# Weight blocks fetched in pairs, and the first units' decays in another order, in a recurrent attention kernel with an ELU network

## Chip, core, metric

The kernel runs on one core of a Trainium2 chip. The metric is the device time of one execution in microseconds (us). The profile is one execution, taken by the hardware profiler; its times count from the start of its span.

## What is computed

```
f = 1 / (1 + exp(-f_logit))                      # q, k, v, f: 4 x 8 x 768 x 48
for t in range(768):
    state = f[t] * state + outer(k[t], v[t])     # one 48 x 48 state for each of 4 x 8 heads
    y[t]  = q[t] @ state
x   = y with the heads side by side              # 3072 x 384
h   = x @ w_in                                   # w_in 384 x 2048
g   = where(h > 0, h, exp(min(h, 0)) - 1)
out = g @ w_out                                  # w_out 2048 x 384
```

All inputs are float32 but `w_in` and `w_out`, which are float64.

## The kernel before

The tokens are worked in 12 units of 256 (`U`), three for each batch. In a unit the recurrence is done in chunks of 64 tokens (`C`): `gates` makes 1 + exp(-f_logit) on ScalarE, `grow` multiplies it up along the tokens on VectorE (a scan), `fall` takes its reciprocal on VectorE (`nc.vector.reciprocal`, line 636), and `scale` multiplies k by the one and q by the other on GpSimd (POOL, line 626). `transposed` turns k over on TensorE, `advance` forms the state updates, `scores` the q-k products, `mask` keeps the causal ones (VectorE, line 722), `step` adds up the states (line 695), and `outputs` and `carried` (for unit 0 `first_outputs`, line 817) form x, which is copied out of PSUM as tile `xt` (lines 827 and 829).

The heads are in pairs p = 0 to 3. Pairs 0 to 2 hold 48 rows of each head at the partitions `MAIN`; the two heads of the fourth pair (index `NKT`) have their decays in the gaps at both ends of the partitions, and `move` brings them to their place by two DMAs from tile `f` to tile `f` (line 643). Only after that can k and q of that pair be scaled.

The network works on units too: for each pair of 128-wide column blocks j = 0 to 7, `up` (psH, line 949 for unit 0, line 904 for the others), `exped` and `elu` (line 958), and `down` (psM, lines 981 and 1015). One step T of the main loop is half a block: at even T `up` of block T / 2, at odd T `down` of a block two earlier. `at_step(T, ...)` puts other work at a step; the tables A1, A2, A3 and D2, D3 say at which. All runs in one order written out by hand (a manual schedule): each engine works its instructions in the order in which the program issues them.

The float64 weights are fetched into a staging tile `area` of 7 slots of 128 x 768 float64, and turned into float32 in three operations, in order of need n = 0 to 15 (w_in blocks 0, 1, 2, then w_out 0, w_in 3, w_out 1 and so on):

- `split(n)`: two VectorE operations (lines 568 and 572), the first into `bits`, the second in place
- `lower(n)`: one ScalarE activation in place (line 578)
- `merge(n)`: one VectorE operation into `wi` or `wo` (line 586), after which, in `fetch`, block n + 7 is fetched into the slot that has become free

A w_in block takes three DMAs (384 rows by 256 columns, runs of 2 KB: `MAIN` 576 KB, and twice 96 KB into the gaps), a w_out block one (768 KB). All come from SP's queue, in program order. Blocks 0 and 1 (`HOLD`) are fetched before unit 1's k, q and v are down; blocks 2 to 6 only after a small GpSimd memset of the staging slots (line 1142). A DMA that is issued takes one of eight completion semaphores in turn, on SP's queue and ACT's together, and waits until the last DMA on that semaphore has landed.

Later the slots of `area` serve again: for `combos` (sums of w_out, line 872) and `mixes` (sums of w_in, line 885), which units 1 to 11 use in place of some of the products.

Before the main loop stands the start-up: unit 0's whole recurrence, the decays of unit 1, and the first two weight blocks. `warm` issues products of an identity that nobody reads (psW, lines 1072 and 1074), whole ones or, by its third argument, tiny ones.

The start-up's last part, before:

```python
    fall(1, 0)
    split(0)
    for c in range(NC - 1):
        step(0, c)
    lower(0)
    mask(0, pc)
    step(0, NC - 1)
    fall(1, 1)
    split(1)
```

Of the kernel before, what the change touches and what calls it, by code (L numbers as in the profile page):

```python
# [356 lines left out]
def fast(ctx: ExitStack, tc: tile.TileContext, q, k, v, f_logit, w_in, w_out, out, flag, outer):  # L357
# [18 lines left out]
    nc = tc.nc  # L376
# [18 lines left out]
    LAG = 2  # L395
    AHEAD = 7
    WA = 1
    F1 = 3
    W0 = 3
    SMALL = 16  # L400
    MORE = 3
    RR = 2
    HOLD = 2
    A1 = (2, 8, 10, 11)
    D2 = (16, 18, 20, 22)
    A2 = (23, 25, 25, 26, 27, 28)
    D3 = (-7, -5, -3, -1)
# [60 lines left out]
    nc.scalar.preload_act_table(AF.Exp)  # L468
    blank(0, nc.vector, nc.gpsimd)
    blank(1, nc.vector, zeros=nc.gpsimd)  # L470
    load(0, "fkq")
    load(1, "f")
    load(0, "v")

    fine = cst.tile([128, NKT, 1], FP32, name="fine")
    nc.vector.memset(fine[:], 1.0)
# [39 lines left out]

    area = cst.tile([128, AHEAD, 2 * DM], w_in.dtype, name="area") if wide else None
    if wide:
        combos = [area[:, i].bitcast(FP32).rearrange("p (n f) -> p n f", f=DH) for i in (5, 6, 0, 1)]
    else:  # L520
        apart = cst.tile([128, 4, NP, DH], FP32, name="combos")
        combos = [apart[:, i] for i in range(4)]

    mixes = cst.tile([128, NP, 4, 128], FP32, name="mixes") if not wide else (
        area[:, 2:5].bitcast(FP32).rearrange("p a f -> p (a f)")[:, 0 : NP * 512]
        .rearrange("p (n c f) -> p n c f", n=NP, c=4)
    )

# [7 lines left out]
    )  # L536
    parts = [need[1:] for need in needs]

    def fetch(n):
        if n >= NFT:  # L540
            return
        j, out_ = parts[n]
        c = slice(j * 256, (j + 1) * 256)
        to = wo[:, 2 * j : 2 * j + 2] if out_ else wi[j][:]
        if wide:
            raws[n] = area[:, n % AHEAD]
            to = raws[n].rearrange("p (k f) -> p k f", k=to.shape[1])
        if out_:
            nc.sync.dma_start(out=to, in_=w_out[c, :].rearrange("(n p) f -> p n f", n=2))
            return  # L550
        nc.sync.dma_start(out=to[MAIN], in_=w_in[0 : NKT * 2 * D, c].rearrange("(k q) f -> q k f", k=NKT))
        rest = w_in[NKT * 2 * D :, c].rearrange("(r d k) f -> r d k f", r=2, d=PAD)
        for r in range(2):
            nc.sync.dma_start(out=to[GAP[r] : GAP[r] + PAD], in_=rest[r])

    held = {}

# [19 lines left out]
    def merge(n):  # L580
        if wide and n < NFT:
            hi = raws.pop(n).bitcast(I32)[:, 1::2]
            j, out_ = parts[n]
            to = wo[:, 2 * j : 2 * j + 2] if out_ else wi[j][:]
            bits, hi = (x.rearrange("p (k f) -> p k f", k=to.shape[1]) for x in (held.pop(n)[:], hi))
            nc.vector.tensor_tensor(out=to.bitcast(I32), in0=bits, in1=hi, op=ALU.add)
        fetch(n + AHEAD)

# [23 lines left out]
    def gates(u, pieces=(NKT,), bias=1):  # L612

        p = 0
        for n in pieces:
            a = qkf[u % NB]["f"][:, p : p + n, 0]
            nc.scalar.activation(a, a, AF.Exp, scale=-1.0)
            if bias:
                nc.scalar.activation(a, a, AF.Copy, bias=1.0)
            p += n  # L620

    def scale(u, *todo):

        t = qkf[u % NB]
        for n, p, e in todo:
            e.tensor_tensor(out=t[n][:, p], in0=t[n][:, p], in1=t["f"][:, p, "kq".index(n)], op=ALU.mult)  # L626

    def grow(u, p):

        g = qkf[u % NB]["f"][:, p, 0]  # L630
        nc.vector.tensor_tensor_scan(out=g, data0=g, data1=g, initial=1.0, op0=ALU.mult, op1=ALU.max)

    def fall(u, p):

        f = qkf[u % NB]["f"]
        nc.vector.reciprocal(f[:, p, 1], f[:, p, 0])  # L636

    def move(u, which, queue):

        f = qkf[u % NB]["f"]  # L640
        for r in range(2):
            to = PAD + D * r
            queue.dma_start(out=f[to : to + D, NKT, which], in_=f[GAP[r] : GAP[r] + PAD, 0:NKT, which])

    def decays(u, p):
        grow(u, p)
        fall(u, p)
        scale(u, ("k", p, nc.gpsimd))
        if p:
            scale(u, ("q", p - 1, nc.gpsimd))  # L650
        if p == NKT - 1:
            move(u, slice(0, 2), nc.sync if u > 1 else nc.scalar)

    def watch(u):
        nc.vector.scalar_tensor_tensor(
# [421 lines left out]


    gates(0, (1, 2))
    fetch(0)  # L1080
    load(1, "kqv")
    for n in range(1, HOLD):
        fetch(n)
    warm(W0, "m3")
    for p in range(NKT):
        grow(0, p)
        scale(0, ("k", p, nc.gpsimd))
        if p < 2:
            transposed(0, 0, "m0", (p,))
    move(0, 0, nc.scalar)  # L1090
    transposed(0, 1, "m1", (0,))
    fall(0, 0)
    scale(0, ("q", 0, nc.gpsimd))
    warm(WA, "m3")
    gates(1, bias=0)
    advance(0, (0, 1))
    pc = scores(0, ("m2", "m3"), (0,))
    nc.gpsimd.tensor_copy(
        even_v[:, :, :, PAD:],
        vs[0][:, :, PAD : PAD + NKT * 2 * D].rearrange("t w (p r d) -> t w p r d", r=2, d=D)[:, :, :, 0],  # L1100
    )
    fall(0, 1)
    scale(0, ("k", NKT, nc.gpsimd), ("q", 1, nc.gpsimd))
    fall(0, 2)
    move(0, 1, nc.scalar)
    warm(4)
    transposed(0, 1, "m1", (1,))
    advance(0, (2,))
    scores(0, None, (1,), pc)
    scale(0, ("q", 2, nc.gpsimd))  # L1110
    advance(0, (3,))
    scores(0, None, (2,), pc)
    nc.gpsimd.tensor_copy(
        padded_v[:, :, :, PAD : 2 * PAD].rearrange("t w (r j) k -> t w r j k", r=2),
        vs[0][:, :, PAD + NKT * 2 * D : PAD + DM].rearrange("t w (r k j) -> t w r j k", r=2, j=NKT),
    )
    a = qkf[1]["f"][:, 0:NKT, 0]
    nc.vector.tensor_scalar_add(a, a, 1.0)
    for p in range(NKT):
        grow(1, p)  # L1120
    move(1, 0, nc.sync)
    scale(0, ("q", NKT, nc.gpsimd))
    warm(2)
    scores(0, None, (NKT,), pc)
    warm(1)
    fall(1, 0)
    split(0)
    for c in range(NC - 1):
        step(0, c)
    lower(0)  # L1130
    mask(0, pc)
    step(0, NC - 1)
    fall(1, 1)
    split(1)
    for c in range(NC - 1):
        nc.gpsimd.tensor_copy(
            padded_s[:, c, :, PAD : 2 * PAD],
            sts[0, c + 1][:, NKT * 64 + PAD : (NKT + 1) * 64].rearrange("p (k j) -> p j k", j=NKT),
        )

    if wide:
        nc.gpsimd.memset(area[:, HOLD:].bitcast(I32)[:, :, 0:1], 0)
    for n in range(HOLD, AHEAD):
        fetch(n)
    merge(0)
    first_outputs(0)
    first_outputs(1)
    lower(1)
    scale(1, ("k", 0, nc.gpsimd), ("q", 0, nc.gpsimd), ("k", 1, nc.gpsimd), ("k", 2, nc.gpsimd))
    scale(1, ("k", NKT, nc.gpsimd))  # L1150
    fall(1, 2)
    watch(0)
    watch(1)
    scale(1, ("q", 1, nc.gpsimd), ("q", 2, nc.gpsimd))
    at_step(A1[2], lambda: outputs(1, ("m3", "m0")), lambda: lower(A1[2]), lambda: lower(A1[2] + 1))
    for n in range(1, NFT):
        t = min(max(needs[n][0] - 2, 0), n) + 2 * (n == NFT - 1)
        if t != A1[1]:
            at_step(t, lambda n=n: merge(n))
        if n > 1:  # L1160
            later.setdefault(max(min(t, n) - 2, 0), []).append(n)
    at_step(F1, lambda: move(1, 1, nc.scalar))
    at_step(F1 + 2, lambda: scale(1, ("q", NKT, nc.gpsimd)))
    at_step(A1[0], lambda: transposed(1, 0, "a0"), lambda: transposed(1, 1, "a1"))
    at_step(4, lambda: warm(0, "m3", SMALL))
# [97 lines left out]
```

## Time and profile before

| | us |
|---|---|
| median of 3 runs | 559.49 (558.94 to 560.98) |
| the profiled execution | 559.46 |
| its span | 557.7 |
| start-up, to the first psH | 30.28 |
| TensorE busy in the span | 543.0 |
| VectorE busy in the span | 406.4 |
| mean granted clock of TensorE | 0.994 |

The span is what the profile's engines show; some 1.8 us lie around it. A line of the timeline gives start and length in us, engine, line of the program, operation, tile written and tiles read, and, in brackets, how long the engine had been idle and what released it. DMA is counted by its 16 engines' busy share and by the GB/s that they moved.

### The profile page before, as it was taken

The numbers are of one execution on the slowest core, as the hardware profiler recorded it, in microseconds if no ns is written. First come the engines' busy times: TensorE is split into PE (matmuls) and PEld (weight loads), VectorE is DVE, ScalarE is ACT, GpSimd is POOL, SyncE is SP. The second block draws the span as 40 slices with busy tenths as digits, with TensorE's granted clock in tenths as the row PEclk, the third lists the DMA queues.
The fourth block names the chain that finished last, engine by engine and source line by source line (L and its number), as shares of the span: only waits on it lengthen the run. The fifth ranks groups of instructions, "written<-read, shape, count | busy, mean of one in ns | idle before, by whom it ended". The sixth has DMA issues, their size and how long they took to land.

```text
span 557.7 us, 15617 instructions
## 1 busy us (share of the span) xinstructions
PE 543.0 (97%) x6358; PEld 507.9 (91%) x6358; DVE 406.4 (73%) x804; ACT 228.3 (41%) x443; POOL 287.8 (52%) x559
## 2 busy tenths in 40 slices
PE   7889999999999999999999999999999999999996
PEld 3477679999999999999999999999999999999996
DVE  8799888887676776786785785786686687745553
ACT  3279764333434343333434334343343344333331
POOL 6600786475473474375465366357258258325332
PEclk9899999999999999999999999999999999999998
DMA  8998971033035135216217207307307302301001
GB/s 211 261 264 214 278 184 43 4 84 88 3 82 146 30 76 149 63 34 186 68 22 186 81 9 192 87 8 192 86 9 191 88 9 72 88 5 33 31 2 35
DMA packets 39474, 54.30 MB, mean 97 GB/s; under 512 B 4032, under 2 KB 29216, under 8 KB 39392
## 3 DMA queue, kind: packets, MB, share of 16 engines
q1 hardware_dynamic: 38592, 52.61, 36.5%
q8 instruction: 52, 0.85, 0.6%
q10 hardware_dynamic: 800, 0.59, 0.4%
q14 instruction: 30, 0.25, 0.2%
HBM read 45.02 MB, written 4.72 MB: 89 GB/s over the span
## 4 chain that ended last, share of the span: by engine, by line
PE 91%; DMA 2%; DVE 2%; ACT 1%; POOL 1%; issue 1%; SPq 1%; ACTq 0%; DVEq 0%; POOLq 0%
PE psH L904 39%; PE psM L1015 37%; PE psM L981 3%; PE psH L949 2%; PE psY L752 2%; PE psY L772 2%; PE psU_a L737 2%; PE psS L714 2%; PE psT L674 1%; DMA area<-in_moe_w_out_dram 1%; DMA f<-f 1%; ACT area L578 1%; DVE f L636 1%; POOL q L626 1%; DMA f<-in_f_logit_dram 0%
## 5 line engine op out<-in xcount | busy, mean ns | idle before, releaser
L904 PE MATMUL psH<-xt,wi 128*128 128x128 f32 (+1 forms) x1056 | 195.0, 294 | 0.0
L968 POOL TENSOR_TENSOR sums<-gg 128x128 f32<-128x128 f32 x172 | 75.6, 460 | 207.8 <-DVE gg L958 188.1
L936 ACT ACTIVATE gg<-hh 128x512 f32<-128x512 f32 x88 | 55.5, 630 | 249.3 <-DVE hh L926 111.7
L904 PEld LDWEIGHTS psH<-xt,wi 128*128 128x128 f32 x1056 | 149.5, 192 | 1.6
L904 PE MATMUL psH<-xt,area 128*128 128x128 f32 x704 | 121.5, 275 | 0.0
L904 PEld LDWEIGHTS psH<-xt,area 128*128 128x128 f32 x704 | 106.5, 192 | 4.5
L913 DVE TENSOR_TENSOR hh<-psH,u 128x256 f32<-128x256 f32 x88 | 36.9, 419 | 97.8 <-ACT u L911 97.7
L1015 PE MATMUL psM<-area,sums 128*128 128x192 f32 x516 | 99.9, 326 | 0.0
L1015 PEld LDWEIGHTS psM<-area,sums 128*128 128x128 f32 x516 | 86.0, 190 | 0.3 <-issue 0.2
L1015 PE MATMUL psM<-wo,gg 128*128 128x192 f32 x376 | 77.7, 332 | 0.0
L958 DVE SCALAR_TENSOR_TENSOR gg<-gg,hh 128x512 f32<-128x512 f32 x88 | 63.8, 725 | 1.5 <-ACT gg L937 1.5
L636 DVE RECIPROCAL f<-f 128x256 f32<-128x256 f32 x36 | 62.7, 1747 | 1.3
L937 ACT ACTIVATE gg<-gg 128x512 f32<-128x512 f32 x96 | 60.6, 631 | 3.0
L1015 PEld LDWEIGHTS psM<-wo,gg 128*128 128x128 f32 x376 | 60.2, 190 | 1.3
L926 DVE TENSOR_TENSOR hh<-psH,u43h 128x256 f32<-128x256 f32 (+1 forms) x176 | 54.6, 352 | 3.0
L626 POOL TENSOR_TENSOR q<-q,f 128x256 f32<-128x256 f32 x48 | 39.6, 826 | 19.5 <-DMA f<-f 12.9
L968 POOL TENSOR_TENSOR sums<-gg,sums 128x128 f32<-128x128 f32 x86 | 45.4, 528 | 6.7
L626 POOL TENSOR_TENSOR k<-k,f 128x256 f32<-128x256 f32 x48 | 39.3, 821 | 10.2 <-DMA f<-f 8.3
L926 DVE TENSOR_TENSOR u43h<-psH,hh 128x256 f32<-128x256 f32 x88 | 37.0, 420 | 9.2 <-PE psH L904 8.7
L968 POOL TENSOR_TENSOR sums<-sums,gg 128x128 f32<-128x128 f32 x86 | 43.0, 500 | 0.0
L1015 PE MATMUL psM<-area,gg 128*128 128x192 f32 x172 | 42.0, 326 | 0.0
L1015 PE MATMUL psM<-wo,sums 128*128 128x192 f32 x172 | 42.0, 326 | 0.0
(102 smaller groups left out, 646.3 us busy)
## 6 DMA issues: line engine op xcount, KB each, us to landing
area<-in_moe_w_out_dram SPq DMA_DIRECT2D x8, 768.0 KB, 10.6
again<-in_moe_w_in_dram SPq DMA_DIRECT2D x16, 384.0 KB, 3.6
again<-in_moe_w_out_dram SPq DMA_DIRECT2D x16, 384.0 KB, 3.6
k<-in_k_dram SPq DMA_DIRECT2D x12, 384.0 KB, 4.5
q<-in_q_dram SPq DMA_DIRECT2D x12, 384.0 KB, 5.6
v<-in_v_dram SPq DMA_DIRECT2D x12, 384.0 KB, 5.8
area<-in_moe_w_in_dram SPq DMA_DIRECT2D x8, 576.0 KB, 8.3
out_dram<-o SPq DMA_DIRECT2D x42, 96.0 KB, 2.4
```

The costliest lines, as they stand in the source:

```text
L626: e.tensor_tensor(out=t[n][:, p], in0=t[n][:, p], in1=t["f"][:, p, "kq".index(n)], op=ALU.mult)
L636: nc.vector.reciprocal(f[:, p, 1], f[:, p, 0])
L714: nc.tensor.matmul(pc[r][FULL[b], w, p], lhsT=t["k"][FULL[r], p, cols], rhs=t["q"][FULL[r], p, cols], start=True, stop=True,)
L904: nc.tensor.matmul(to, lhsT=lhs, rhs=rhs, start=(n == 0), stop=True, skip_group_check=True)
L913: add = lambda to, x, y: nc.vector.tensor_tensor(out=to, in0=x, in1=y, op=ALU.add)
L926: add = lambda to, x, y: nc.vector.tensor_tensor(out=to, in0=x, in1=y, op=ALU.add)
L936: nc.scalar.activation(g[:], h, AF.Relu, scale=-1.0)
L937: nc.scalar.activation(g[:], g[:], AF.Exp, scale=-1.0)
L958: nc.vector.scalar_tensor_tensor(out=g[:], in0=g[:], scalar=-1.0, in1=phs.pop(P), op0=ALU.add, op1=ALU.max)
L968: nc.gpsimd.tensor_tensor(out=s[:, i], in0=x, in1=y, op=op)
L981: nc.tensor.matmul(pm[t][:], lhsT=g[:, i, t * 128 : (t + 1) * 128], rhs=wo[:, 2 * j + i, :], start=(j == 0 and i == 0), stop=(j == NP - 1 ...
L1015: nc.tensor.matmul(pm[bank][:, half * DH : (half + 1) * DH], lhsT=x, rhs=y, start=first, stop=(j == NP - 1), skip_group_check=True,)
```

## The change

- `fetch` is called by kind and block. w_in comes in pairs of blocks: three DMAs bring 96 rows by 512 columns each, into two neighbouring slots (runs of 4 KB in the weight, 2 KB in each slot), and four the gaps of both. A table gives each pair and each w_out block its slot; `combos` and `mixes` lie at other slots accordingly.
- The order of SP's transfers is another. Unit 0's v comes ahead of unit 1's f; no w_in goes out ahead of the first `move`; unit 1's k follows the first two pairs, then unit 1's `move`, w_out 0 and 1, unit 1's q and v, w_out 2, the third pair, w_out 3, the fourth pair. w_out 7 is fetched after the loads of unit 2, which are themselves issued at step 8 as before.
- The first `move` uses ACT's and SP's queue, one DMA each. The second (of the reciprocals of the fourth pair) is gone: `fall(0, NKT)` takes the reciprocal in place.
- All three `fall` of unit 1 come in the main loop (steps 1, 3 and 4), with the q products that follow them; before, one came after the first psH was due. Unit 1's second `move` is at step 4, unit 1's transposes at step 4 instead of 2.
- Unit 1's "+ 1" is an activation on ScalarE instead of a VectorE operation.
- `mask` and all `step` of unit 0 stand ahead of `split(0)` and `split(1)`. `merge(2)` is at step 1.
- Fewer whole `warm` products in the start-up (7 calls' worth instead of 11); two more tiny ones at step 4, three more at step 22. The memset is gone.

```diff
-    F1 = 3
+    F1 = 4
-    SMALL = 16
-    MORE = 3
+    SMALL = 18
+    MORE = 6
-    HOLD = 2
-    A1 = (2, 8, 10, 11)
+    A1 = (4, 8, 10, 11)
...
-    load(0, "fkq")
+    load(0, "fkqv")
     load(1, "f")
-    load(0, "v")
...
-        combos = [area[:, i].bitcast(FP32).rearrange("p (n f) -> p n f", f=DH) for i in (5, 6, 0, 1)]
+        combos = [area[:, i].bitcast(FP32).rearrange("p (n f) -> p n f", f=DH) for i in (3, 0, 1, 2)]
...
-        area[:, 2:5].bitcast(FP32).rearrange("p a f -> p (a f)")[:, 0 : NP * 512]
+        area[:, 4:7].bitcast(FP32).rearrange("p a f -> p (a f)")[:, 0 : NP * 512]
...
+    spots = {("in", 0): 0, ("in", 2): 2, ("in", 4): 0, ("in", 6): 2}
+    spots.update({("out", j): i for j, i in enumerate((4, 5, 6, 4, 5, 0, 1, 2))})
+
+    def fetch(kind, j):
+        i = spots[kind, j]
+        if kind == "out":
...
+            return
         if wide:
+            for h in range(2):
+                raws[parts.index((j + h, 0))] = area[:, i + h]
+            to, c = area[:, i : i + 2].rearrange("p h (k f) -> p k h f", k=NKT), slice(j * 256, (j + 2) * 256)
+            for k_ in range(NKT):
+                rows = slice(k_ * 2 * D, (k_ + 1) * 2 * D)
+                nc.sync.dma_start(out=to[MAIN, k_], in_=w_in[rows, c].rearrange("q (h f) -> q h f", h=2))
...
+    after = {
+        1: (("out", 2),), 5: (("in", 6), ("out", 4)), 8: (("out", 5), ("out", 6)), 12: (("out", 7),),
+    }
...
-        fetch(n + AHEAD)
+        for what in after.get(n, ()):
+            fetch(*what)
...
     gates(0, (1, 2))
-    fetch(0)
-    load(1, "kqv")
-    for n in range(1, HOLD):
-        fetch(n)
...
-    move(0, 0, nc.scalar)
+    move(0, 0, (nc.scalar, nc.sync))
+    fetch("in", 0)
+    fetch("in", 2)
+    load(1, "k")
+    for p in range(2):
+        transposed(0, 0, "m0", (p,))
...
-    gates(1, bias=0)
+    gates(1)
...
-    fall(0, 2)
-    move(0, 1, nc.scalar)
-    warm(4)
...
+    warm(1)
+    fall(0, NKT)
+    scale(0, ("q", NKT, nc.gpsimd))
+    scores(0, None, (NKT,), pc)
...
-    a = qkf[1]["f"][:, 0:NKT, 0]
-    nc.vector.tensor_scalar_add(a, a, 1.0)
-    for p in range(NKT):
-        grow(1, p)
-    move(1, 0, nc.sync)
-    scale(0, ("q", NKT, nc.gpsimd))
-    warm(2)
-    scores(0, None, (NKT,), pc)
-    warm(1)
-    fall(1, 0)
+    grow(1, 0)
+    mask(0, pc)
+    for c in range(NC):
+        step(0, c)
     split(0)
-    for c in range(NC - 1):
-        step(0, c)
-    lower(0)
-    mask(0, pc)
-    step(0, NC - 1)
-    fall(1, 1)
-    split(1)
+    grow(1, 1)
+    grow(1, 2)
+    move(1, 0, (nc.sync, nc.sync))
+    fetch("out", 0)
+    fetch("out", 1)
+    load(1, "qv")
...
-    if wide:
-        nc.gpsimd.memset(area[:, HOLD:].bitcast(I32)[:, :, 0:1], 0)
-    for n in range(HOLD, AHEAD):
-        fetch(n)
+    split(1)
+    first_outputs(0)
+    lower(0)
     merge(0)
-    first_outputs(0)
     first_outputs(1)
     lower(1)
...
-    fall(1, 2)
...
+    at_step(1, lambda: fall(1, 0), lambda: scale(1, ("q", 0, nc.gpsimd)), lambda: merge(2))
...
-    at_step(F1, lambda: move(1, 1, nc.scalar))
+    at_step(F1 - 1, lambda: fall(1, 1), lambda: scale(1, ("q", 1, nc.gpsimd)))
+    at_step(F1, lambda: fall(1, 2), lambda: scale(1, ("q", 2, nc.gpsimd)))
+    at_step(F1, lambda: move(1, 1, (nc.scalar, nc.scalar)), lambda: fetch("in", 4), lambda: fetch("out", 3))
```

More of the change, by code (lines that the diff above doesn't have):

```diff
@@ L537, in fast @@
     parts = [need[1:] for need in needs]
-    def fetch(n):
-        if n >= NFT:
+    spots = {("in", 0): 0, ("in", 2): 2, ("in", 4): 0, ("in", 6): 2}
[3 more added lines that the diff above has]
+        if kind == "out":
+            to = wo[:, 2 * j : 2 * j + 2]
+            if wide:
+                to = area[:, i].rearrange("p (k f) -> p k f", k=2)
+                raws[parts.index((j, 1))] = area[:, i]
+            nc.sync.dma_start(out=to, in_=w_out[j * 256 : (j + 1) * 256, :].rearrange("(n p) f -> p n f", n=2))
@@ L541, in fetch @@
             return
-        j, out_ = parts[n]
-        c = slice(j * 256, (j + 1) * 256)
-        to = wo[:, 2 * j : 2 * j + 2] if out_ else wi[j][:]
         if wide:
[L546 to L551, printed above, removed]
@@ L552, in fetch @@
-        rest = w_in[NKT * 2 * D :, c].rearrange("(r d k) f -> r d k f", r=2, d=PAD)
-        for r in range(2):
-            nc.sync.dma_start(out=to[GAP[r] : GAP[r] + PAD], in_=rest[r])
+            for h in range(2):
[4 more added lines that the diff above has]
+                nc.sync.dma_start(out=to[MAIN, k_], in_=w_in[rows, c].rearrange("q (h f) -> q h f", h=2))
@@ new lines, in fetch @@
+        for h in range(2):
+            to, c = area[:, i + h].rearrange("p (k f) -> p k f", k=NKT) if wide else wi[j + h][:], j + h
+            c = slice(c * 256, (c + 1) * 256)
+            if not wide:
+                nc.sync.dma_start(
+                    out=to[MAIN], in_=w_in[0 : NKT * 2 * D, c].rearrange("(k q) f -> q k f", k=NKT)
+                )
+            rest = w_in[NKT * 2 * D :, c].rearrange("(r d k) f -> r d k f", r=2, d=PAD)
+            for r in range(2):
+                nc.sync.dma_start(out=to[GAP[r] : GAP[r] + PAD], in_=rest[r])
@@ L636, in fall, with move @@
         nc.vector.reciprocal(f[:, p, 1], f[:, p, 0])
-    def move(u, which, queue):
+    def move(u, which, queues):
         f = qkf[u % NB]["f"]
@@ L642, in move @@
             to = PAD + D * r
-            queue.dma_start(out=f[to : to + D, NKT, which], in_=f[GAP[r] : GAP[r] + PAD, 0:NKT, which])
+            queues[r].dma_start(out=f[to : to + D, NKT, which], in_=f[GAP[r] : GAP[r] + PAD, 0:NKT, which])
     def decays(u, p):
@@ L651, in decays @@
         if p == NKT - 1:
-            move(u, slice(0, 2), nc.sync if u > 1 else nc.scalar)
+            move(u, slice(0, 2), (nc.sync, nc.sync))
     def watch(u):
@@ L1087, in fast @@
         scale(0, ("k", p, nc.gpsimd))
-        if p < 2:
-            transposed(0, 0, "m0", (p,))
-    move(0, 0, nc.scalar)
+    move(0, 0, (nc.scalar, nc.sync))
[4 more added lines that the diff above has]
+        transposed(0, 0, "m0", (p,))
     transposed(0, 1, "m1", (0,))
@@ L1101, in fast @@
     )
+    advance(0, (2,))
+    warm(1)
     fall(0, 1)
-    scale(0, ("k", NKT, nc.gpsimd), ("q", 1, nc.gpsimd))
+    scale(0, ("q", 1, nc.gpsimd), ("k", NKT, nc.gpsimd))
+    scores(0, None, (1,), pc)
+    transposed(0, 1, "m1", (1,))
     fall(0, 2)
-    move(0, 1, nc.scalar)
-    warm(4)
-    transposed(0, 1, "m1", (1,))
-    advance(0, (2,))
-    scores(0, None, (1,), pc)
     scale(0, ("q", 2, nc.gpsimd))
@@ L1112, in fast @@
     scores(0, None, (2,), pc)
+    warm(1)
+    fall(0, NKT)
+    scale(0, ("q", NKT, nc.gpsimd))
+    scores(0, None, (NKT,), pc)
     nc.gpsimd.tensor_copy(
@@ L1139, in fast @@
         )
-    if wide:
-        nc.gpsimd.memset(area[:, HOLD:].bitcast(I32)[:, :, 0:1], 0)
-    for n in range(HOLD, AHEAD):
-        fetch(n)
+    split(1)
+    first_outputs(0)
+    lower(0)
     merge(0)
-    first_outputs(0)
     first_outputs(1)
     lower(1)
-    scale(1, ("k", 0, nc.gpsimd), ("q", 0, nc.gpsimd), ("k", 1, nc.gpsimd), ("k", 2, nc.gpsimd))
-    scale(1, ("k", NKT, nc.gpsimd))
-    fall(1, 2)
+    warm(1)
+    for p in (*range(NKT), NKT):
+        scale(1, ("k", p, nc.gpsimd))
     watch(0)
     watch(1)
-    scale(1, ("q", 1, nc.gpsimd), ("q", 2, nc.gpsimd))
+    at_step(1, lambda: fall(1, 0), lambda: scale(1, ("q", 0, nc.gpsimd)), lambda: merge(2))
     at_step(A1[2], lambda: outputs(1, ("m3", "m0")), lambda: lower(A1[2]), lambda: lower(A1[2] + 1))
@@ L1157, in fast @@
         t = min(max(needs[n][0] - 2, 0), n) + 2 * (n == NFT - 1)
-        if t != A1[1]:
+        if n != 2 and t != A1[1]:
             at_step(t, lambda n=n: merge(n))
```

## The prediction

> **What bounds the kernel now.** I read the page's busy shares and its chain first, then busy times by stage, then the first 75 us on the timeline.
>
> ```profile
> PE 543.0 (97%) x6358; PEld 507.9 (91%) x6358; DVE 406.4 (73%) x804; ACT 228.3 (41%) x443; POOL 287.8 (52%) x559
> PE 91%; DMA 2%; DVE 2%; ACT 1%; POOL 1%; issue 1%; SPq 1%; ACTq 0%; DVEq 0%; POOLq 0%
> ```
>
> TensorE is the bound over the whole span, so only time in which it does no needed work can be won. The stages (columns: PE, PEld, DVE, ACT, POOL busy, clock, DMA share, GB/s) tell where that is:
>
> ```profile
> 0.00:30.30 30.30, 22.23 (x327) 11.66 (x327) 23.84 (x32) 9.69 (x17) 18.20 (x46) 0.94 0.96 237
> 30.30:43.50 13.20, 12.61 (x85) 9.89 (x85) 11.74 (x18) 11.07 (x11) 0.74 (x1) 1.00 1.03 259
> 43.50:58.30 14.80, 14.04 (x233) 10.47 (x233) 14.18 (x24) 11.30 (x11) 0.88 (x1) 1.00 0.85 221
> 111.10:557.70 446.60, 441.36 (x5130) 431.26 (x5128) 310.81 (x660) 165.98 (x359) 231.42 (x452) 1.00 0.29 76
> ```
>
> After 111 us TensorE is full and the change touches nothing there. Until 30.3 us its busy time is partly fillers (psW). From 30.3 to 58.3 us VectorE is busy 25.9 of 28.0 us: TensorE and VectorE are nearly level there. Lines of the timeline (start, length):
>
> ```profile
> 16.48 0.72 POOL L626 TENSOR_TENSOR k<-k,f 128x256 f32<-128x256 f32 x1 [4.88 <-DMA f<-f]
> 23.43 1.29 DVE L722 TENSOR_TENSOR at<-psS,twice 128x512 f32<-128x512 f32 x2 [3.47 <-PE psS L714]
> 44.44 0.95 DVE L586 CUSTOM_DVE_ANT_0 wo<-area,bits 128x1536 uint16<-128x1536 uint16 x1
> 70.78 0.56 DVE L568 TENSOR_SCALAR bits<-area 128x768 int32<-128x768 int32 x1
> ```
> ```profile
> 19.57 3.35 PE L1074 MATMUL psW<-ident 128*128 128x512 f32 x4
> 22.85 0.46 PE L714 MATMUL psS<-q,k 64*64 64x64 f32 x16
> 30.28 2.86 PE L949 MATMUL psH<-xt,wi 128*128 128x256 f32 x12 [1.67 <-DVE xt L829]
> 46.15 2.74 PE L981 MATMUL psM<-wo,gg 128*128 128x384 f32 x8
> ```
>
> To see: the last scores need the gap heads' decay, which a DMA f<-f brings (4.88 us wait), and stand behind fillers at half clock; the mask waits 3.47 us for them; the first useful product of the second stage starts at 30.28. The second psM (46.15) follows a VectorE merge that ends at 45.39. Up to 45.4 VectorE is busy 37.44 us, so idle 7.96.
>
> **What the Trainium skill says.** "TensorE: Matmul & The Clock Gate", part 1: the clock is full or half, by activity in free-running windows of 3413 ns. The trace agrees: TensorE was busy 1.50 us in 15.52:18.93, then
>
> ```profile
> 18.93:22.35 3.41, 3.40 (x20) 1.69 (x20) 0.99 (x3) 2.00 (x2) 3.41 (x9) 0.50 1.06 213
> ```
>
> "SBUF — State Buffer" (ports): VectorE and GpSimd lock a shared port pair. The trace agrees: the L572 half of a split takes 0.97 us at 18.34 beside GpSimd, 0.56 us at 38.34 alone. "DMA: Bandwidth & Descriptors" ("Issuing engines are not separate DMA queues"): SP's and ACT's transfers share the same 16 engines. Agrees: ACT's 48 KB f<-f takes 4.6 to 5.4 us from issue to landing while w_in streams.
>
> **The change part by part** (n counts weight blocks in order of need: 0, 1, 2, 4, 6 of w_in; 3, 5, 7 of w_out; 15 the last).
>
> *Gap heads' decay.* The shift of f (L643, two DMAs) is issued at 8.5 on ACT and SP, not at 10.15 and 10.91 on ACT, and no w_in lies ahead of it, only f and v of the first loads, down by 11.1: it lands at about 11.7, not 16.35. The second shift (two DMAs, 98 KB, 1.2 us of ACT's queue) becomes a fourth reciprocal on VectorE, +1.65. On SP all w_in now waits for the scan that ends at 8.43: first issue 9.1 instead of 6.17. Nothing is lost: engines are busy with first loads until 11.1.
>
> *Walk to the first psH.* VectorE: scans to 8.43, four reciprocals (4.94 for three, 1.65) to 14.95, one scan of unit 1 to 15.6 (its +1 goes to ACT: VectorE -0.62, ACT about +0.85, idle there). q times decay on POOL (0.73) to 15.8, psS (0.46), mask starts at 16.4, not 23.43. Mask 1.21, three adds 0.38 each, product 0.28: 19.0. Split 1.06, two scans 1.24, split 1.06: 22.4. Merge 0.93, xt copy 0.58: psH at 23.9, a lead of 6.4. Checks: w_in lands from 11.7 at about 0.25 MB/us, 1.4 MB by 17.3, before the split at 19.0; lower(0) on ACT runs 20.1 to 22.0, xt copies on ACT to 23.0, all before the merge's end. Warm-ups: 7 instead of 11, none at half clock if the windows hold.
>
> *What is given back.* All three reciprocals of unit 1 (L636, 1.67 from start to start) now follow psH; one did before. VectorE from the merge of n=1: it waits for lower (L578, 1.9) until 24.95, merge 25.9; split with POOL's k products beside it 27.2; reciprocal 28.9; lower(2) stands behind gg on ACT (28.1 to 30.0), merge(2) 31.0, split(3) 32.1, ELU 32.7, split(4) 33.8, lower(3) done 34.1, merge(3) 35.1, reciprocal 36.8, split(5) 37.9, ELU 38.6, merge(4) 39.5, reciprocal 41.2, split(6) 42.3, merge(5) 43.3. psH2 waits for the ELU that frees its PSUM, psH3 for merge(4), second psM for merge(5): 43.35 against 46.15, **2.8 us** ahead. So of 6.4 the VectorE queue takes back 3.6. The transposes at step 4 (were 2) need k1, landed by 25.5, and POOL's four products, done by 28.7: in time.
>
> *Transfers.* A pair costs 7 issues instead of 6; w_in is read in runs of 4 KB. SP's shift of unit 1 waits for the scans (21.3) and holds w_out, q and v behind it; pair 2 and k1, in flight to 25.5, cover that. Block 6 now has 10.2 MB up to its end (it had 8.8). At the rate of
>
> ```profile
> 4.50:44.00 39.50, 34.11 (x412) 21.29 (x412) 32.98 (x45) 19.98 (x27) 15.35 (x32) 0.96 1.04 258
> ```
>
> with 0.45 MB down at 4.5, it lands at 4.5 + 9.75/0.258 = 42.3; needed at 41.2. An estimate: runs of w_out's kind went at 286 GB/s (window 49:68), so 4 KB runs may give some 5%: 40.5. I take it as just in time; the bounds are 39 and 44.5 (w_in alone at 240). Block 15 (n=15) goes behind the 1.67 MB of unit 2: 7.7 MB after block 6 at 0.286 is 27 us, plus about 1.5 for a lane that waits on ACT's shift: 70 to 71, against 68.7. Its split stands at 70.78 now and would at 68; psH8 needs it only some 3.6 us later (split, ELU, merge, ELU), at 73.3 to 76.1, so up to about 71 it costs little.
>
> *Small ones.* ACT's shift of unit 1 waits for the last reciprocal (41.2) with kn copies and gg2 behind it: merge(6) is due 2 us later than that needs. SMALL +2 falls into the wait for psH2: nothing, 0.12 if that cover is gone. MORE +3 at step 22: 3 x 0.06 = +0.2 on TensorE. The POOL memset (0.1) goes: nothing. Moved staging slots: all read after their last merge: nothing; bounds -0.3 to +0.3.
>
> Sum: -2.8 + 0.2 = -2.6. Profiled execution 559.46 (span 557.7 and 1.8 around it; the median of the runs is 559.49, so no correction): 556.9.
>
> **Rivals.**
> 1. *VectorE is relieved more.* Of its 7.96 idle only 4.0 must stay (start 2.3, scores 0.8, lower 0.9), the new work is 1.03, and 1.8 of port contention (split, split, merge) goes: -4.7, 554.8. For: 6.4 us of lead. Against: two more reciprocals where it is level with TensorE, and transfers.
> 2. *The lead is swallowed.* Block 6 lands at 44.5: second psM at 46.6, no gain, 559.5. For: DMA share 1.04 in that stretch.
> 3. *Slower: block 15 late.* If pairs run no faster and lanes leave 3 to 4 us of gaps, it lands at 75; split, ELU, merge, ELU put psH8's second half at 78.6 against 76.1: +2.5 to +3, 562.2. It decides from a landing after 72.5.
> 4. *The pairs change nothing*: packets stay 2 KB since the two halves go to two slots. Then 2, or 1.5 off.
>
> **Numbers.** What a measurement tells from none is 0.5%, 2.8 us. Main case 0.52 (own range 555.3 to 558.3, 0.24 of the 0.52 under 556.7); rival 1 0.20; rivals 2 and 4 0.14; rival 3 0.14. Faster 0.20 + 0.24 = 0.44, same 0.28 + 0.14 = 0.42, slower 0.14. Range 553.8 to 561.5.
>
> **What would show it.** Right: mask near 16.4, first psH at 23.5 to 24.7, TensorE idle 1 to 2 us each before psH2, psH3 and the second psM, VectorE without a gap there, second psM at 43 to 44.5, then the same distances. Wrong: psH after 26; VectorE waiting for DMA area at split(6) or for block 15; a half-clock window after 24 us; any difference after 111 us.

## The result: slower, 1.0049 times the time before

| | before | after |
|---|---|---|
| median (lowest to highest), us | 559.13 (557.43 to 560.98), 22 runs | 561.27 (559.42 to 564.72), 22 runs |
| ratio, 95% interval | | 1.0049 (1.0034 to 1.0064) |
| the profiled execution, us | 559.46 | 560.88 |
| first psH, second psM, fifth psH, psH8 | 30.28, 46.15, 50.84, 75.19 | 25.08, 47.26, 53.52, 76.88 |
| start of the last psM | 545.51 | 547.04 |
| blocks n = 6 and 15 landed | 40.04, 68.72 | 45.07, 73.05 |
| mean granted clock of the runs | 0.997 to 0.998 (the runs beside the experiments) | 0.993 |

The interval lies wholly above 1, so the change is slower; 0.49%, some 2.7 us, is just under the 0.5% that the prediction named as what can be told from none. psH8 is the first psH of unit 1's network and the starts are read from the timeline. The changed kernel begins its useful products 5.2 us sooner and is 2.7 us late by the fifth psH; from psH8 to the last psM the distance to before hardly changes (1.7 to 1.5 us).

The profile after, busy time and chain over the whole span:

```profile
PE 540.5 (97%) x6360; PEld 506.4 (91%) x6360; DVE 406.5 (73%) x804; ACT 229.6 (41%) x444; POOL 288.3 (52%) x558
PE 90%; DMA 7%; DVE 1%; POOL 1%; SPq 0%; issue 0%; DVEq 0%; POOLq 0%
```

TensorE still bounds the span, but DMA has gone from 2% of the chain to 7%: some 28 us more of the chain that a transfer takes up. By stage (PE, PEld, DVE, ACT, POOL busy, clock, DMA share, GB/s):

```profile
0.00:25.08 25.08, 17.50 (x318) 9.51 (x318) 20.42 (x30) 10.54 (x18) 13.53 (x39) 1.00 0.92 214
25.08:37.06 11.98, 10.59 (x81) 8.52 (x81) 9.57 (x14) 7.52 (x8) 3.52 (x5) 1.00 0.97 308
37.06:53.52 16.46, 11.93 (x157) 7.80 (x157) 14.20 (x19) 12.11 (x11) 2.37 (x3) 0.90 0.91 227
```

The loss is in the third line: 16.46 us of which TensorE is busy 11.93, at a mean clock of 0.90. The lines of the timeline that answer to those shown of before, VectorE first; the second is `split(6)`, whose line of before is

```profile
43.37 0.56 DVE L568 TENSOR_SCALAR bits<-area 128x768 int32<-128x768 int32 x1
```

and the lines after are:

```profile
16.88 1.29 DVE L735 TENSOR_TENSOR at<-psS,twice 128x512 f32<-128x512 f32 x2 [1.48 <-PE psS L727]
45.19 0.56 DVE L580 TENSOR_SCALAR bits<-area 128x768 int32<-128x768 int32 x1 [1.99 <-DMA area<-in_moe_w_in_dram]
73.14 0.56 DVE L580 TENSOR_SCALAR bits<-area 128x768 int32<-128x768 int32 x1 [0.61 <-DMA area<-in_moe_w_out_dram]
```
```profile
25.08 5.45 PE L962 MATMUL psH<-xt,wi 128*128 128x256 f32 x24 [0.83 <-DVE xt L842]
47.26 4.30 PE L994 MATMUL psM<-wo,gg 128*128 128x384 f32 x8 [2.75 <-DVE wo L598]
```

The mask comes 6.5 us sooner, as the edit means it to. But `split(6)` waits 1.99 us for a transfer (none before) and `split(15)` 0.61 us, and the second psM takes 4.30 instead of 2.74 us: half clock. The 2.7 us at the fifth psH are 1.1 of a later second psM and 1.6 of half clock behind it. The windows of 3.41 us show why:

```profile
43.40:46.81 3.41, 1.12 (x6) 0.64 (x4) 1.59 (x3) 2.21 (x5) 0.61 (x1) 1.00 0.69 224
46.82:50.23 3.41, 2.97 (x5) 1.76 (x6) 3.34 (x5) 3.41 (x3) 0.73 (x1) 0.50 0.81 211
```

In the first TensorE was busy 1.12 us, since it waited for the merge behind the late split; in the next the clock is 0.50. Where the late split comes from is in the chain of waits between 27 and 55 us (start, length, what):

```profile
27.91 8.34 DMA v<-in_v_dram
36.25 0.02 issue
36.26 8.80 DMA area<-in_moe_w_in_dram
...
45.19 0.57 DVE bits L580
```

A gap DMA of the third pair was issued at 36.26, the moment unit 1's v had landed: it waited for a completion semaphore, and landed at 45.07. The chain names this wait, but the wait is not what made the block late. The pair's last `MAIN` DMA, issued already at 30.30, landed at 44.45; the gap DMA issued at 35.35 landed at 44.77 and the one issued at 36.26 at 45.07. They landed in the order of issue, behind bytes that were in the queue long before. The transfer engines had work until 42.5:

```profile
26.50:28.00 1.50, 1.50 (x9) 1.32 (x8) 1.14 (x3) 0.02 (x1) 0.00 (x0) 1.00 0.55 90
28.00:42.50 14.50, 11.33 (x80) 8.13 (x79) 13.16 (x15) 9.77 (x8) 4.44 (x6) 1.00 1.04 314
42.50:45.07 2.57, 2.02 (x10) 1.43 (x8) 0.70 (x1) 0.51 (x2) 0.72 (x1) 1.00 0.50 92
```

Semaphores show in the first of these lines: w_out 0 was issued only at 26.45, when the w_in DMA eight places ahead of it had landed (26.43), and for 1.5 us the engines were little more than half busy. The third line is the end of the pair itself, for which `split(6)` waits.

### The profile page after: what moved, and what is told of

Its sections match the earlier page's. It is cut to its first block, busy times and chain, and to the rows that moved or that the text cites. A ratio compares the mean times of both kernels' runs of the same rounds, so it can differ in the third digit from the quotient of the medians.

```text
span 559.1 us, 15615 instructions
## 1 busy us (share of the span) xinstructions
PE 540.5 (97%) x6360; PEld 506.4 (91%) x6360; DVE 406.5 (73%) x804; ACT 229.6 (41%) x444; POOL 288.3 (52%) x558
## 3 DMA queue, kind: packets, MB, share of 16 engines
q1 hardware_dynamic: 38720, 52.66, 35.3%
## 4 chain that ended last, share of the span: by engine, by line
PE 90%; DMA 7%; DVE 1%; POOL 1%; SPq 0%; issue 0%; DVEq 0%; POOLq 0%
PE psH L917 39%; PE psM L1028 37%; DMA area<-in_moe_w_in_dram 5%; PE psM L994 4%; PE psY L765 2%; PE psY L785 2%; PE psU_a L750 2%; PE psH L962 2%; PE psS L727 2%; DMA v<-in_v_dram 1%; PE psT L687 1%; DMA k<-in_k_dram 1%; POOL k L639 0%; DVE o L1038 0%; DVE wo L598 0%
## 5 line engine op out<-in xcount | busy, mean ns | idle before, releaser
L649 DVE RECIPROCAL f<-f 128x256 f32<-128x256 f32 x37 | 64.4, 1746 | 1.2
```

## The experiments

Three theories at the start: **A**, the third pair's landing sets the second psM; **B**, the three reciprocals in VectorE's queue set it; **C**, the half-clock window costs a large part of the time. D, E and F came later and are named in the expectations. Each kernel is the changed one with the edit shown. All ratios are to the kernel before, run beside it (6 to 22 executions of each kernel); "clock" is the mean granted clock over the kernel's runs, the other columns are of its profiled execution. That is one execution, and not always a typical one: in e7, e10 and e12 it was the fastest of its kernel, in e2 the slowest. So the ratio says what an edit is worth, and the other columns where it acts.

| kernel | block 6 landed | second psM | fifth psH | block 15 landed | psH8 | clock | ratio (95%) |
|---|---|---|---|---|---|---|---|
| before | 40.04 | 46.15 | 50.84 | 68.72 | 75.19 | 0.998 | 1 |
| after | 45.07 | 47.26 | 53.52 | 73.05 | 76.88 | 0.993 | 1.0049 (1.0034 to 1.0064) |
| e1 third pair first | 42.01 | 44.71 | 51.64 | 76.20 | 78.41 | 0.992 | 1.0058 (1.0035 to 1.0081) |
| e2 single blocks | 46.47 | 49.15 | 56.86 | 75.59 | 80.47 | 0.993 | 1.0052 (1.0035 to 1.0070) |
| e3 filler at step 7 | 45.16 | 47.36 | 52.16 | 73.04 | 75.52 | 0.996 | 1.0017 (1.0004 to 1.0031) |
| e4 no reciprocals | 44.87 | 47.78 | 52.58 | 74.83 | 76.98 | 0.992 | 1.0073 (1.0058 to 1.0088) |
| e5 last block first | 43.59 | 45.79 | 52.22 | 69.38 | 75.59 | 0.994 | 1.0015 (1.0003 to 1.0027) |
| e6 both moved | 42.13 | 44.80 | 52.16 | 68.38 | 77.21 | 0.996 | 1.0004 (0.9988 to 1.0020) |
| e7 old transfers | 40.38 | 45.49 | 52.66 | 68.84 | 76.02 | 0.992 | 1.0045 (1.0033 to 1.0057) |
| e8 = e7 + filler | 40.52 | 48.88 | 53.58 | 70.01 | 76.94 | 0.993 | 1.0033 (1.0020 to 1.0045) |
| e9 = e7, no reciprocals | 40.16 | 44.93 | 49.63 | 68.09 | 73.00 | 0.994 | 1.0004 (0.9992 to 1.0016) |
| e10 = e7 + shift sooner | 40.20 | 46.04 | 50.74 | 69.09 | 74.53 | 0.994 | 1.0024 (1.0015 to 1.0033) |
| e11 = e6 + shift sooner | 42.34 | 45.16 | 49.86 | 66.02 | 73.22 | 0.995 | 0.9997 (0.9981 to 1.0012) |
| e12 = e11 + filler | 41.84 | 44.27 | 48.97 | 65.26 | 72.33 | 0.998 | 0.9998 (0.9987 to 1.0009) |
| f1 fillers, two places | 44.71 | 46.92 | 51.73 | 71.20 | 75.09 | 0.997 | 1.0029 (1.0015 to 1.0042) |
| f2 shift sooner | 46.02 | 48.77 | 53.57 | 75.82 | 77.92 | 0.994 | 1.0061 (1.0039 to 1.0083) |

0.001 of a ratio is 0.56 us.

### The third pair

e1 issues the third pair ahead of w_out 2:

```diff
-        1: (("out", 2),), 5: (("in", 6), ("out", 4)), 8: (("out", 5), ("out", 6)), 12: (("out", 7),),
+        5: (("in", 6), ("out", 4)), 8: (("out", 5), ("out", 6)), 12: (("out", 7),),
...
-    at_step(F1, lambda: move(1, 1, (nc.scalar, nc.scalar)), lambda: fetch("in", 4), lambda: fetch("out", 3))
+    at_step(F1, lambda: move(1, 1, (nc.scalar, nc.scalar)), lambda: fetch("in", 4), lambda: fetch("out", 2), lambda: fetch("out", 3))
```

> The changed kernel with one edit: the third pair of w_in (blocks n = 6 and 8) is issued ahead of w_out 2 (n = 7) instead of behind it. Theory A (the third pair's landing sets the second psM): block 6 lands about 3 us earlier (768 KB at 0.27 MB/us), near 42 instead of 45.1; VectorE's wait of 1.99 us at split(6) shrinks below 0.5, the second psM starts near 45.3 instead of 47.26, and the time falls by 1.5 to 3 us against the changed kernel. Rival B (VectorE's own queue, with the three reciprocals after psH, sets it): nothing moves by more than 0.5 us. Rival C (the half-clock window alone costs the time): the second psM may move, the time only where no half-clock window follows.

Theory A holds for its own point: block 6 landed 3 us sooner and the second psM came 2.5 us sooner. One profile each could be chance, but with the third pair first (e1, e6, e11, e12) block 6 landed at 41.8 to 42.3, and with the order of the change (after, e3, e4, e5, f1, f2) at 43.6 to 46.0. The time did not follow. Two other transfers were next. Timeline of e1, VectorE and TensorE:

```profile
76.29 0.74 DVE L580 TENSOR_SCALAR bits<-area 128x768 int32<-128x768 int32 x1 [4.50 <-DMA area<-in_moe_w_out_dram]
```
```profile
51.25 0.46 PE L727 MATMUL psS<-q,k 64*64 64x64 f32 x16 [1.90 <-POOL q L639]
78.41 0.79 PE L917 MATMUL psH<-xt,wi 128*128 128x128 f32 x2 [3.24 <-DVE gg L971]
```

The last block landed at 76.20 and psH8 stood 3.24 us behind it; and unit 1's last scores waited 1.90 us for the scaled q, which waits for unit 1's second decay shift (two DMAs, issued on ACT at 42.06 and 42.68, the later landed at 50.33).

e2 undoes the pairs, in the same places of the order, so that w_in is read again in runs of 2 KB:

```diff
-            for k_ in range(NKT):
-                rows = slice(k_ * 2 * D, (k_ + 1) * 2 * D)
-                nc.sync.dma_start(out=to[MAIN, k_], in_=w_in[rows, c].rearrange("q (h f) -> q h f", h=2))
...
-            if not wide:
...
+            nc.sync.dma_start(
+                out=to[MAIN], in_=w_in[0 : NKT * 2 * D, c].rearrange("(k q) f -> q k f", k=NKT)
+            )
```

> The changed kernel with the pairs undone: each place of a pair in SP's order fetches its two blocks one after the other, with three DMAs each (runs of 2 KB in the weight), in the same slots. If the pair's longer runs make w_in faster, this is slower by up to 2 us and the first four blocks land later than 27.8. If the pairs bring nothing and only put the second block's bytes ahead of the first block's end (theory A), block 0 lands some 1.5 us earlier than 18.7 and block 6 some 2 us earlier than 45.1, and the time falls by 1 to 2.5 us.

The first four blocks were down at 26.7 with single blocks. With pairs it was 27.8 in the change and 25.3 to 27.9 in the profiles of kernels that are the same up to there, so this shows no difference. The ratio is that of the change. The pairs bring nothing that shows, nor do they cost what was lost; the second expectation failed too, for block 6 landed at 46.47, no sooner.

e4 leaves out unit 1's three reciprocals (its decays are not inverted, their tile is set to 1):

```diff
+    nc.gpsimd.memset(qkf[1]["f"][:, 0:NKT, 1], 1.0)
     grow(1, 0)
...
-    at_step(1, lambda: fall(1, 0), lambda: scale(1, ("q", 0, nc.gpsimd)), lambda: merge(2))
+    at_step(1, lambda: scale(1, ("q", 0, nc.gpsimd)), lambda: merge(2))
...
-    at_step(F1 - 1, lambda: fall(1, 1), lambda: scale(1, ("q", 1, nc.gpsimd)))
-    at_step(F1, lambda: fall(1, 2), lambda: scale(1, ("q", 2, nc.gpsimd)))
+    at_step(F1 - 1, lambda: scale(1, ("q", 1, nc.gpsimd)))
+    at_step(F1, lambda: scale(1, ("q", 2, nc.gpsimd)))
```

> The changed kernel without the three reciprocals of unit 1's decays (5.2 us of VectorE): their tile is set to 1 by one GpSimd memset in the start-up, so unit 1's q products are not divided by the decays. Rival B (VectorE's queue sets the second psM): it starts near 43 and the time falls by 2.5 to 4 us. Theory A: VectorE comes to split(6) by 39 and waits there until 45.1; the second psM stays at 46.8 to 47.5 and the time falls by less than 1 us.

```profile
45.30 0.56 DVE L580 TENSOR_SCALAR bits<-area 128x768 int32<-128x768 int32 x1 [4.95 <-DMA area<-in_moe_w_in_dram]
```

VectorE had 5 us less to do and waited 4.95 us instead of 1.99 for the same transfer. B falls: while the third pair is late, VectorE's queue is not what sets the second psM. The time did not fall, as A had said it would a little; the ratio is higher than that of the change, with intervals that overlap, and why is open.

### The half clock

e3 puts two products of 128x512 that nobody reads into the wait:

```diff
+    at_step(7, lambda: warm(2, "m3"))
```

> The changed kernel with two whole filler products more (1.7 us at full clock) at step 7, between the third psH and the second psM, where TensorE waits. Rival C (the half-clock window after that wait costs 1.6 us): no half-clock window between 43 and 54, the stretch from the second psM to the fifth psH takes 4.7 instead of 6.26, and the time falls by 1 to 1.6 us. Theory A or B alone: the time stays, since the second psM starts when it did.

The landings and waits stayed (`split(6)` waited 2.26 us), the window after 43 us kept full clock, and the ratio fell by 0.0032, with intervals apart. f1 also turns the 18 tiny fillers of step 4 into two whole ones, which takes the half-clock window out of the stretch that e3 had at 34.8:

```diff
-    at_step(4, lambda: warm(0, "m3", SMALL))
+    at_step(4, lambda: warm(2, "m3"))
+    at_step(7, lambda: warm(2, "m3"))
```

> The changed kernel with fillers alone altered: two 128x512 products at step 4 in place of the 18 small ones, and two more at step 7. Nothing of its transfers, VectorE's queue or its shift is touched. Theory C (half clock is most of the loss): the mean granted clock of the runs rises from 0.993 to 0.997 or more, and the time falls to 559.0 to 559.8 us, though the third pair still lands near 45 and its split waits 2 us, and the last block still lands near 73. Rival (the waits themselves are the loss): the clock rises but the time stays at 560.3 to 561.3.

The clock rose to 0.997 as expected; the ratio, 1.0029, lies between C and its rival. Fillers alone thus give back some 0.0020 to 0.0032 of 0.0049 (the two kernels' intervals overlap), about half. The runs of the changed kernel agree: its five runs at a clock of 0.988 to 0.989 took 563.3 to 564.7 us, its one at 1.000 took 559.42, and a line through all 22 gives 0.39 us for 0.001 of clock. That is a correlation; e3 and f1 are the interventions, and only e3's gain is clear of the change's interval.

The profile of the change hides a second such place. In ten of the thirteen profiles of kernels with the changed start-up and the tiny fillers at step 4, a half-clock window begins between 33.3 and 35.7, at the third psH; the change's own, e2 and e6 have none there. So e11:

```profile
29.91:33.32 3.41, 2.12 (x44) 1.45 (x42) 2.88 (x5) 1.05 (x2) 0.90 (x2) 1.00 1.10 298
33.32:36.73 3.41, 3.39 (x8) 2.77 (x9) 3.38 (x4) 2.65 (x4) 1.46 (x2) 0.50 1.06 252
```

The two kernels with whole fillers there (f1, e12) show none, and have the highest mean clocks of all kernels with the changed start-up.

### The last block

e5 issues unit 2's loads behind w_out 7 instead of ahead of it:

```diff
-    at_step(8, lambda: load(2))
+    at_step(13, lambda: load(2))
```

> The changed kernel, with the loads of unit 2 (1.67 MB) issued behind the last block w_out 7 instead of ahead of it. Theory C (half clock and the third pair set the loss, the late last block is covered by ELU and merge slack): w_out 7 lands at 66 to 69 instead of 73.05, the split of the last block no longer waits (0.61 before), but psH8 stays within 0.5 us of 76.9 and the time stays at 560.8 to 561.3 us. Theory D (the late last block is what keeps the loss from being worked off): psH8 comes at 75.2 to 75.9 and the time falls to 559.5 to 560.2. If unit 2's inputs become late instead, a wait of k, v or f of unit 2 on VectorE or GpSimd shows after 78 us and the time rises.

Block 15 landed at 69.38 and its split waited no more; psH8 came at 75.59, as D said; the ratio fell from 1.0049 to 1.0015, with intervals apart: 1.9 us. (That its block 6 landed at 43.59 is not the edit's doing, which acts only behind it; so psH8 of this one profile is in part chance.) No wait for unit 2's inputs shows at psH8.

e6 makes both moves, e1's and e5's:

> Both moves together: third pair ahead of w_out 2, and w_out 7 ahead of unit 2's loads. If the third pair alone failed to pay only because the last block came at 76.20 (its split waited 4.5 us), then w_out 7 lands at 69 to 71.5, the split of the last block waits under 0.5 us, psH8 comes at 74.5 to 76 and the time falls to 558 to 560 us. If instead the scores' wait for unit 1's second decay shift (1.90 us in the run with the third pair first) and the half clock after it set the end, psH8 stays at 77 to 78.5 and the time at 561 to 562.5.

Against e1 the last block alone is worth 0.0054, 3.0 us. Against e5 the third pair's move is worth nothing clear of noise. The time is that of before, although psH8 in the profiled execution (77.21) came later than expected: there the scores waited 2.33 us for the shift and a half-clock window followed at 53.19. At 561.71 us it was one of the slowest of the 14.

### The decay shift of unit 1

e7 keeps the changed start-up and takes the transfers of before: single blocks in order of need, a ring of seven slots, block n + 7 fetched after `merge(n)`.

```diff
-        for what in after.get(n, ()):
-            fetch(*what)
+        fetch(n + AHEAD)
...
-    fetch("in", 0)
-    fetch("in", 2)
+    fetch(0)
     load(1, "k")
+    fetch(1)
+    fetch(2)
+    fetch(3)
...
-    fetch("out", 0)
-    fetch("out", 1)
+    fetch(4)
     load(1, "qv")
+    fetch(5)
+    fetch(6)
...
```

> The changed kernel's start-up (decays inverted in place, masks ahead of splits, reciprocals and loads of unit 1 as they are there) with the transfers of before: single blocks in order of need, seven slots in a ring, each slot refilled after the merge of its block, mixes and sums in the slots of before. Theory A (order of transfers loses the lead): block 6 lands at 42 to 43.5 and the last block at 68 to 70, the split of block 6 waits under 0.5 us, the first psH stays at 24 to 25.5, the second psM comes at 43.5 to 45.2 and the time is 556.5 to 558.5 us, faster than both. Rival: the engines' queues and the sum of bytes set the start-up whatever the order; then the second psM comes at 46 to 47.5 and the time is 559 to 561.5.

The part of A that made it the whole cause falls. All blocks were on time (block 6 at 40.38, block 15 at 68.84), and the ratio stayed at 1.0045. The chain of e7:

```profile
43.87 6.98 DMA f<-f
...
51.01 1.21 POOL q L621
...
52.27 0.46 PE psS L709 x16
52.73 2.79 PE psH L944 x12
```

The last reciprocal of unit 1 ends at 43.2, its shift needs 7 us, q must be scaled, and only then can the scores ahead of the fifth psH end. e8 adds e3's filler to e7:

> The same with two filler products at step 7. If TensorE stays at full clock after 24 us without it, it costs 0 to 0.9 us against the run without; if there is a half-clock window there, it saves 1 to 1.6 us.

Its profiled execution had three half-clock windows after 25 us in spite of the filler; the gain, 0.0012, is within the intervals. e10 moves the last two reciprocals and the shift one step sooner:

```diff
-    F1 = 4
+    F1 = 3
```

> As the run with the old transfers, with unit 1's last two reciprocals and its second decay shift one step sooner (F1 3 instead of 4, as before the change). Theory F (in that run the late shift, landing at 50.45 and 50.85, set the fifth psH): the shift lands at 45 to 47.5, the gap heads' scores no longer wait (2.13 us), the second psM comes at 45.5 to 46.5, the fifth psH at 50.2 to 51.2 and the time is 559.3 to 560.5 us. If TensorE falls to half clock once more after 24 us it stays 1.3 above that. Rival: the shift isn't what decides; fifth psH at 52 to 53, time 561.5 to 562.5.

Fifth psH at 50.74, 1.9 us sooner, though the second psM came 0.55 us later: the scores no longer waited. The ratio is 0.0021 lower, the intervals only just touching, so some 1.2 of e7's 2.5 us go with this edit, which moves two reciprocals along with the shift. It is not all: e6's shift landed as late (50.56, against 50.85 in e7) and e6 runs as before. Its mean clock is 0.996, e7's 0.992; at 0.39 us for 0.001 that would be some 1.6 of the 2.3 us between the two, an estimate. The rest is open. The same edit alone on the changed kernel is f2:

> The changed kernel with unit 1's last two reciprocals, its second decay shift and the issue of the third pair one step sooner (F1 3 instead of 4). Theory F (the shift is one of several limits, and not the one that binds while the third pair lands at 45): the fifth psH comes within 1 us of 53.5 and the time is 560.3 to 561.5 us. Rival (the late shift alone is the loss): fifth psH at 50 to 51.5, time 559 to 559.8.

It gives nothing (six runs; the time came above the range): its third pair landed at 46.02 and its last block at 75.82, and that these bind first is argued, not tested.

### All limits together, and what is left

e9 is e7 without unit 1's reciprocals, so without the late shift too:

> The changed kernel's start-up with the transfers of before (single blocks in order of need), and unit 1's three reciprocals left out: its decays are not inverted, and the tile that should hold them is set to 1. This takes away both the 5 us of VectorE and the late second shift that the scores waited for (2.13 us). Theory E (the weight transfers bound the whole stage to 76 us, not only block 6): blocks 12 and 15 still land at about 61.2 and 69, so the fifth psH comes at 47 to 50 but VectorE then waits for the blocks at 54 and 61, psH8 at 74 to 75.2, and the time is 558.0 to 559.5 us. Rival: the queues of the engines bound the stage; then the lead of some 3 us is kept to the end, psH8 at 71.5 to 73, time 555.5 to 557.5.

```profile
39.65 7.76 DMA area<-in_moe_w_in_dram
...
47.53 0.99 DVE bits L563
...
50.52 10.72 DMA area<-in_moe_w_in_dram
...
61.36 0.58 DVE bits L563
```

E holds for the time: 5 us of VectorE's work and the shift's wait are gone, and the time is that of before (1.0004). psH8 (73.00) came sooner than E said and stands at the rival's edge, so it doesn't decide; and its lead of 2.2 us does not last. The next products wait 0.78 us for xt, which GpSimd makes, and the last psM (544.36) is only 1.15 us ahead of before. The chain shows w_in transfers twice, into `split(8)` and `split(12)`. Before the change `split(12)` stood at 61.73 and its block landed at 61.19: 0.5 us of slack was all there was.

e11 has both moves of e6 and the sooner shift, e12 also f1's filler at step 4:

> Both transfers moved (third pair ahead of w_out 2, w_out 7 ahead of unit 2's loads), and the same step sooner for unit 1's last reciprocals and shift. Theory F: fifth psH at 50 to 51 instead of 52.16, block 12 at 57.5 to 60, last block at 67 to 69, psH8 at 75 to 76, time 558.0 to 559.3. Rival: time as without, 559.3 to 560.2, since the second psM comes later by what the scores gain.

> The run with both transfers moved and the shift one step sooner had a half-clock window at 33.32 to 36.73 us (its third psH took 4.52 instead of 2.86 us). Here the 18 small fillers of step 4 (36 records of 128x1, 1.04 us) become two 128x512 products (0.6 us each), in the same wait. If the clock then stays full after 24 us, the third psH takes 2.86 us and the chain behind it comes sooner as far as the transfers allow: block 12 landed there at 55.60 and was split at 61.22, so they allow it: 556.5 to 557.8 us, 0.2 to 0.5% under before. If the merges of VectorE set the chain anyway (TensorE waited 1.78 us for a merge after that window), it stays at 557.8 to 559.3 us, no difference from before.

Both run as fast as the kernel before, no faster. From block 12 on, e11's dates came 1 to 2 us sooner than expected (psH8 at 73.22), without gain over before. e12's clock is 0.998, as before, and its profiled execution starts the last psM 1.7 us sooner than that of before; but at 557.58 us that was the fastest of its 22 executions, and the median, 559.22, shows no gain. What takes the 1.7 us back in the others was not seen in a profile and stays open.

## Why the prediction was wrong, point by point

The step that failed is the landing of the weights. The sum used the rate of all transfers, 258 GB/s, for the block's own, which was 0.235 to 0.240 MB/us, so it had block 6 at 42.3 instead of 45.07. That wait, and a VectorE walk that came 2.0 us late, took the lead of 2.8 us away. What made the kernel slower than before are two terms that the sum put at little or nothing: the last block (1.9 us by e5) and the half clock (1.8 us by e3; the two overlap).

- **First psH at 23.9: nearly right.** The shift landed at 11.34 (11.7 was said), the mask stood at 16.88 (16.4), psH at 25.08: a lead of 5.2 instead of 6.4.
- **VectorE takes back 3.6: too little.** The fourth psH came at 41.69, and the last reciprocal ended at 43.2 where the walk had 41.2; of these 2.0 us the later first psH is 1.2. Without the 1.99 us wait the second psM would have stood at 47.26 - 1.99 = 45.3 by estimate, a lead of 0.9 instead of 2.8.
- **Block 6 "just in time": this step failed.** It landed at 45.07, where the sum had 42.3 and the upper bound 44.5. The 258 GB/s of the sum are what all transfers moved, those behind the block included. By the prediction's own bytes, what stood up to the end of block 6 came down before at (8.8 - 0.45)/(40.04 - 4.5) = 0.235 MB/us, and after at (10.2 - 0.45)/(45.07 - 4.5) = 0.240: the block's own rate hardly changed. With the 0.235 of before the sum gives 4.5 + 9.75/0.235 = 46.0. So the landing was mis-sized by 2.8 us, and VectorE waited for it. e1 agrees: w_out 2's 0.79 MB, taken from ahead of the block, are 3.3 us at 0.240, and it landed at 42.01. The semaphores (the prediction's lanes), counted for block 15 and not here, are a small part: the thin 1.5 us at 26.5 to 28.0, at a share of 0.55 instead of 1.04, are some 0.7 us, an estimate. No run changed their number. Rival 2, which had the landing at 44.5, was right here.
- **Block 15 "costs little": mis-sized, and a large part of the loss.** Said: 70 to 71. Measured: 73.05, and 71.20 to 76.20 in the kernels that keep unit 2's loads ahead of it. From block 6 to block 15 the prediction had 27 + 1.5 us and 27.98 were measured: in the change the lateness is block 6's, handed on. Rival 3's mechanism, place and point of decision (72.5) hold: e5 puts 1.9 us on the last block and e6 against e1 3.0 us, where it said 2.5 to 3. It had been given 0.14.
- **ACT's shift "due 2 us later": incomplete.** It named `merge(6)` as what is late next; it was the scores. In the changed kernel the late third pair hid it; where that was gone, the scores waited (1.90 us in e1, 2.33 in e6, 2.13 in e7).
- **The half clock was in no sum.** It was named only as a sign of being wrong. e3 and f1 put 1.1 to 1.8 us on it, f1's part within the intervals. The Trainium skill, "TensorE: Matmul & The Clock Gate", "Why this matters for your kernels", asks for no gaps of TensorE above about 3 us; here the longest gap was 2.75 us, and the measurement decides: a window with 1.12 us of work was followed by half clock.
- **Rival 4 was right:** w_in's packets are 2 KB in both kernels, and e2 shows that the pairs' form decides nothing.
- **Rival 1 fell:** e4 and e9 took still more from VectorE, and neither came under the time of before.

The losses don't add up: the late block 6 takes the lead away, the last block and the half clock make the loss, and e3 and e5, which each give back more than half, overlap. The chance of slower, 0.14, had this case as one mishap. In the profile of before, block 6 landed 3.3 us ahead of its split, block 12 0.5 and block 15 2.1; a change that moves all of them has more ways to lose than one.

## What to carry to other kernels

A lead at the start is worth no more than the least slack of the later arrivals that don't come sooner with it: list for each transfer its landing against its use before a prologue is made shorter, and do it also for small ones such as the shift of 48 KB here. When transfers are reordered, add up the bytes ahead of each block, and divide them by the rate at which a block's own queue came down, not by the rate of all that moved; a chain that names a semaphore's wait has not shown that the transfer would have landed sooner. Look at the last block of a stream: 1.67 MB ahead of it cost 1.9 us here. Where a stage starves TensorE, price a half-clock window for every window left mostly idle, and try a filler in the wait first; it is the cheapest experiment.

## What was not expected of the hardware

- A single wait of 2.75 us, in a window with 1.12 us of TensorE work, brought half clock for 3.41 us; 18 tiny fillers (36 records of 128x1, 1.04 us) ahead of the third psH did not keep the clock in e11 (window with 2.12 us busy, tiny ones included); with two whole products e12 kept it.
- The granted clock differs from run to run of one kernel (0.988 to 1.000 after, 0.989 to 1.000 before): one profile doesn't tell how often a marginal window is lost. The profiled execution of the change, at 0.997, was a mild one.
- A DMA of 48 KB from tile to tile (unit 1's second shift) took 3.0 (f1) to 8.1 us (e9) on ACT's queue from issue to landing while weights streamed, and in e7 the scores waited 2.13 us behind it.
